# A Fourier-mixing and maxout kernel: another order of loads, writes and preparations ahead of the first block

## The chip, the cores and the metric

The kernel runs on one core of a Trainium2 chip. The metric is the device time of one execution in microseconds (us), a median over runs. One execution was also recorded by the hardware profiler; its times are those of the trace below.

## The reference

The input x has 8 sequences of 3072 tokens with 256 features. The first part takes the real part of a two-dimensional Fourier transform of each sequence, the second a feed-forward layer with three input matrices and a maximum:

```python
def _attn_ref(x):                       # x: (8, 3072, 256)
    X = np.fft.fft(x, axis=1)
    X = np.fft.fft(X, axis=2)
    return X.real.astype(np.float32)

def _moe_ref(x, w1, w2, w3, w_out):     # w1, w2, w3: (256, 768), w_out: (768, 256)
    h = np.maximum(np.maximum(x @ w1, x @ w2), x @ w3)
    return (h @ w_out).astype(np.float32)
```

The output has 24576 rows of 256 in float32.

## The kernel before, in words

**The transform over the tokens** is done in two stages for each sequence ("block", b from 0 to 7). A token index is split as 32 rows (a) by 96 columns (s); by symmetry only 49 columns (NS) are kept, with the mirrored ones stacked on other partitions. `load_x` fetches x into the tile xt, two loads (h = 0, 1) for each range of columns; `mirror` (lines 126 and 127, DVE) folds the features in half on the second 64 partitions. `Mix.s(k)` multiplies eight columns by the small table tabz (two matmuls of 512 columns) and evicts them on ScalarE (ACT) to the tile tb; s0 to s6 cover the 49 columns. `Mix.y` writes tb to a DRAM buffer db, one DMA for the even and one for the odd columns; `Mix.z` reads it back in another layout, as the tile yb with 98 partitions. So a transposition goes through DRAM. `Mix.u` and `Mix.x0` make a correction for feature 0, which `Mix.c` copies into yb. `Mix.k(which, g)` multiplies yb by a third of the table te_tab or to_tab (1536 columns, in thirds g = 0, 1, 2) and evicts the result to tE or tO. `Mix.end` makes the middle token.

**The tables** are computed on the chip: `angles(c0, c1)` computes angles on DVE for a range of the columns (four instructions), `tables(c0, c1)` makes two sines and an absolute value of them on ACT.

**The transform over the features** is multiplied into the weights once. `product(i, half, jh, ...)` is four matmuls of 384 columns; `keep_product` evicts them: half 0 to gE on DVE or another engine, half 1 to gO on ACT, from which gD is scaled. jh is the half of the 768 hidden columns. The products of jh = 0 come ahead of block 0, those of jh = 1 are the four steps of `prep_first` inside it. `prep_second` has four steps: three times four matmuls with an eviction to g1t, and then twelve matmuls that give gw, with which the linear part of the layer is computed. `load_w(jh)` loads w1, w2, w3 as two halves, from POOL's queue.

**The main loop** runs over 8 blocks, each with three groups (blk) of six units (jc): 18 units a block. A unit is `unit_plus` (four matmuls of 512 columns into the accumulators pse2 and pse3, lines 390 and 391) and `unit_out` (a ReLU of pse2 on ACT into stmp, then a maximum with pse3 on DVE, into hp). One unit later `finish` adds `unit_minus` (two matmuls with gD, line 398) into the same accumulators, which gives the mirrored tokens, and takes the maximum again, into hm. There are two buffers each of pse2 and pse3, so a unit cannot begin before hm of the unit two before it is taken. The second layer's matmuls (lines 429, 437 and 414) of the group before are spread between the units; stores go out from SP's queue and, as scattered rows, from POOL's.

**What sets the order.** The order on each engine's queue is written out by hand: a list `plan` says behind which unit of which block a piece is issued, `at(b, unit, fn)` fills it. Engines run their queues in order; waits are put in by the framework from what is read and written. PSUM has eight banks: ps_f (two buffers) for s, k, x0, end and the preparations' outputs inside the blocks, ps_s (six buffers) only at the beginning, then handed over to the accumulators and to ps_o. The tile warm is in ps_s; `warm_up(n)` issues n matmuls whose result nobody reads. Before the change they multiply the first columns of x:

```python
    def warm_up(n):
        for _ in range(n):
            nc.tensor.matmul(warm, tab_at[0], xt[0][:, 0:8:2, 0:128], start=True, stop=True)
```

For block 0 the loads of x come in four ranges of columns, FIRST = ((0, 16), (16, 32), (32, 40), (40, 49)), and the writes `Mix.y` in the same four. The zeros of the tile zero are written to the end of each row of db once, at the start.

Of the kernel before, what the change touches and what calls it, by code (L numbers as in the profile page):

```python
# [50 lines left out]
def kernel(  # L51
# [123 lines left out]
    zero = gen.tile([128, 256], BF16, tag="zero")  # L175
    nc.vector.memset(zero, 0.0)
    for db in dbs:
        pads = db[:, 64 * 128:].rearrange("s (r c) -> s r c", c=256)
        nc.sync.dma_start(out=pads, in_=zero[0:NS].unsqueeze(1).to_broadcast([NS, 2, 256]))
# [79 lines left out]

    def tables(c0, c1):  # L260
        cs = slice(c0, c1)
        nc.scalar.activation(out=te_tab[:, cs], in_=kvec[:, cs], func=AX.Sin, scale=step)
        nc.scalar.activation(out=q[:, cs], in_=kvec[:, cs], func=AX.Abs)
        nc.scalar.activation(out=to_tab[:, cs], in_=q[:, cs], func=AX.Sin, scale=-step,
                             bias=half_pi)
# [13 lines left out]
    def keep_product(psg, i, half, jh, evict_e):  # L279

        cs = slice(jh * 384, (jh + 1) * 384)
        if half == 0:
            evict_e(out=gE[i][:, cs], in_=psg[:, 0:384])
        else:
            nc.scalar.copy(out=gO[i][:, cs], in_=psg[:, 0:384])
            nc.gpsimd.tensor_scalar(out=gD[i][:, cs], in0=gO[i][:, cs], scalar1=dif,
                                    scalar2=None, op0=ALU.mult)
# [33 lines left out]
    class Mix:  # L321
# [19 lines left out]
        def y(self, s0=0, s1=NS):  # L341
            dst = self.db.rearrange("s (q f) -> q s f", f=128)
            done = []
            for hh in range(2):
                n = (s1 - s0 + 1 - hh) // 2
                done.append(nc.sync.dma_start(
                    out=dst[0:64, s0 + hh:s1:2, :],
                    in_=tbv[hh * 64:hh * 64 + 64, s0 // 2:s0 // 2 + n, :]))
            return done

        def z(self, i0=0, i1=RI, eng=nc.sync):
            rows = self.db.rearrange("s (c q) -> (s c) q", c=2)
            return eng.dma_start(out=yb[0:KS, i0 * 256:i1 * 256], in_=rows[:, i0 * 256:i1 * 256])
# [14 lines left out]
        def k(self, which, g):  # L368
# [6 lines left out]
            nc.scalar.copy(out=(self.tE, self.tO)[which][:, g * 512:(g + 1) * 512], in_=ps2)  # L375
# [159 lines left out]
    def warm_up(n):  # L535
        for _ in range(n):
            nc.tensor.matmul(warm, tab_at[0], xt[0][:, 0:8:2, 0:128], start=True, stop=True)
# [7 lines left out]
    m = Mix(0)  # L545
    m.s(0, pool=ps_s)
    m.s(1, pool=ps_s)
    m.y(0, 16)
    warm_up(3)
# [3 lines left out]
    warm_up(3)  # L553
    m.s(4, pool=ps_s)
    m.y(32, 40)
    warm_up(2)
    m.s(5, pool=ps_s)
    m.s(6, pool=ps_s)
    written = m.y(40, NS)
# [5 lines left out]
    m.z(0, 6)  # L565
    m.z(6, RI)
    load_w(1, written[-1])
    warm_up(4)
# [5 lines left out]
    warm_up(8)  # L574
# [6 lines left out]
    for u in range(3):  # L581
# [10 lines left out]
    nc.gpsimd.dma_start(out=wout_bf.rearrange("p (jc c) -> p jc c", jc=NJC),  # L592
                              in_=moe_w_out.rearrange("(jc p) c -> p jc c", jc=NJC))
    HALVES = ((0, 25), (25, NS))
    for (s0, s1) in HALVES:
        for h in range(2):
            load_x(1, s0, s1, h)

# [7 lines left out]

    m.c(0, 6, nc.scalar.copy)
    m.k(0, 0)
    m.k(1, 0)
# [41 lines left out]
    for (u, fn) in ((1, lambda: next(first)), (1, lambda: next(first)),  # L651
                    (2, lambda: next(first)), (2, lambda: next(first)), (2, lambda: m.c(6, RI)),
                    (2, lambda: m.k(0, 1)), (2, lambda: tables(1024, NHALF + 1)),
                    (3, lambda: m.k(1, 1)), (3, lambda: next(second)), (4, lambda: next(second)),
                    (4, lambda: next(second)), (5, lambda: next(second)),
# [13 lines left out]
    ahead0 = {5: ("s0", "s1"), 6: ("s2", "y0"), 7: ("s3", "s4", "u"), 8: ("s5", "s6", "y1", "x"),  # L669
# [82 lines left out]
```

## Time and profile before

| | |
|---|---|
| median of 3 runs | 422.1 us (421.14 to 423.2) |
| the profiled execution | 420.71 us, of which span 418.9 us |
| mean granted TensorE clock | 0.998 |
| TensorE (PE) busy | 394.4 us, 94% of the span |
| VectorE (DVE) busy | 293.4 us, 70% |
| ScalarE (ACT) busy | 252.8 us, 60% |
| GpSimd (POOL) busy | 154.0 us, 37% |

How to read the rows shown below. In a view in order of time a row gives the start in us, the busy time in us, the engine, the line of the kernel, the operation, output<-input with shapes, how many instructions (x4), and in brackets the idle time of the engine before it with what ended that. PEld is TensorE's load of weights; SPq and POOLq are DMA issues from those queues. A matmul's end is modelled; matmuls are pipelined, so the next one starts before the listed end. In a view by stretches a row gives the stretch, its length, then for PE, PEld, DVE, ACT and POOL the busy time and the number of instructions, the granted clock, the mean share of time in which the 16 DMA engines were busy (above 1 where packets overlap), and GB/s.

### The profile page before, as it was taken

To read this page: it belongs to the slowest core of one execution; us is meant where nothing else is said; L and a number is where in the kernel's file an instruction comes from. 1 tells how busy PE (TensorE), PEld (TensorE's weight loads), DVE (VectorE), ACT (ScalarE), POOL (GpSimd) and SP (SyncE) were. 2 spreads that over 40 slices of the span, in tenths; PEclk is the share of its full clock that TensorE was granted. 3 is DMA by queue.
4 is the path that set the end of the run, shared out by engine and by line. 5 is a ranking of instruction groups with operands and counts; after the bars stand their busy time and mean duration, and the time that the engine had idled before them with its cause. 6 is when DMAs were issued, how large, how long until landed. Compare 5 with 4: busy or idle time off the path is not lost.

```text
span 418.9 us, 8123 instructions
## 1 busy us (share of the span) xinstructions
PE 394.4 (94%) x2732; PEld 247.3 (59%) x2780; DVE 293.4 (70%) x527; ACT 252.8 (60%) x475; POOL 154.0 (37%) x264
## 2 busy tenths in 40 slices
PE   1977789999999999999999999999999999999995
PEld 0334456656665666656665666656665666656664
DVE  6876556866785676856786676856786676667772
ACT  2666656665576656665576656665576656645550
POOL 7381123424532434324532434324442432333430
PEclk9999999999999999999999999999999999999999
DMA  8997237935962569335962569335982552212224
GB/s 123 171 203 124 64 71 183 194 91 113 222 150 67 136 165 199 90 88 112 227 148 64 139 160 194 98 88 115 210 163 66 136 152 75 77 57 66 83 75 125
DMA packets 66443, 53.25 MB, mean 127 GB/s; under 512 B 34661, under 2 KB 62000, under 8 KB 65204
## 3 DMA queue, kind: packets, MB, share of 16 engines
q0 software_dynamic: 23376, 26.27, 32.1%
q1 hardware_dynamic: 42386, 25.95, 23.8%
q10 hardware_dynamic: 640, 0.52, 0.5%
q8 instruction: 21, 0.34, 0.3%
q14 instruction: 20, 0.16, 0.1%
HBM read 35.14 MB, written 31.69 MB: 160 GB/s over the span
## 4 chain that ended last, share of the span: by engine, by line
PE 88%; DVE 4%; DMA 3%; ACT 2%; issue 1%; POOL 1%; DVEq 0%; POOLq 0%; SPq 0%; ACTq 0%
PE po L414 29%; PE pse L390 16%; PE pse L398 14%; PE pse L391 13%; PE ps L333 5%; PE po L437 5%; PE pl L429 3%; PE ps L373 2%; DMA xt<-in_x_dram 2%; DVE xt L126 1%; DVE hm L405 1%; DMA yb<-db 1%; DVE hp L405 1%; PE psg L273 1%; DVE xt L127 1%
## 5 line engine op out<-in xcount | busy, mean ns | idle before, releaser
L404 ACT ACTIVATE stmp<-pse 128x512 bf16<-128x512 f32 x288 | 169.9, 601 | 80.6 <-PE pse L391 60.5
L447 POOL DMA_INDIRECT out_dram<-ot,rows_m x92 | 104.0, 1131 | 236.4 <-DVE ot L442 225.2
L405 DVE TENSOR_TENSOR hp<-pse,stmp 128x512 bf16<-128x512 f32 x144 | 99.6, 691 | 109.5 <-PE pse L398 57.4
L390 PE MATMUL pse<-tE,gE 128*128 128x512 bf16 x286 | 108.4, 379 | 3.3 <-ACT stmp L404 0.9
L405 DVE TENSOR_TENSOR hm<-pse,stmp 128x512 bf16<-128x512 f32 x144 | 99.0, 688 | 1.0 <-ACT stmp L404 0.9
L391 PE MATMUL pse<-tO,gO 128*128 128x512 bf16 x251 | 95.1, 379 | 0.2
L414 PE MATMUL po<-wout_bf,hp 128*128 128x256 bf16 x576 | 86.1, 273 | 0.0
L398 PE MATMUL pse<-tO,gD 128*128 128x512 bf16 x279 | 83.8, 379 | 0.5
L414 PE MATMUL po<-wout_bf,hm 128*128 128x256 bf16 x576 | 78.6, 273 | 0.0
L414 PEld LDWEIGHTS <-hp 128*128 128x128 bf16 x576 | 56.3, 98 | 26.2
L414 PEld LDWEIGHTS <-hm 128*128 128x128 bf16 x576 | 56.3, 98 | 16.4
L442 DVE TENSOR_TENSOR ot<-po,even 128x512 f32<-128x512 f32 x92 | 62.9, 683 | 0.2
L398 PEld LDWEIGHTS <-gD 128*128 128x128 bf16 x288 | 27.6, 98 | 32.1
L335 ACT CAST tb<-ps 128x512 bf16<-128x512 f32 x48 | 26.3, 588 | 28.5 <-PE ps L333 28.5
L391 PEld LDWEIGHTS <-gO 128*128 128x128 bf16 x288 | 28.1, 97 | 23.4 <-issue 2.3
L390 PEld LDWEIGHTS <-gE 128*128 128x128 bf16 x288 | 28.1, 98 | 22.3 <-issue 0.8
L333 PE MATMUL ps<-xt,tabz 128*128 128x512 bf16 x96 | 27.0, 400 | 12.6 <-DVE xt L127 11.2
L437 PE MATMUL po<-gw,tO 128*128 128x512 bf16 x92 | 34.9, 379 | 0.0
L433 ACT COPY even<-pl 128x512 f32<-128x512 f32 x46 | 27.0, 587 | 0.0
L375 ACT CAST tO<-ps 128x512 bf16<-128x512 f32 x24 | 14.0, 585 | 16.5 <-PE ps L373 8.8
L121 POOL DMA_DIRECT2D xt<-in_x_dram x36 | 23.4, 659 | 0.0
L375 ACT CAST tE<-ps 128x512 bf16<-128x512 f32 x24 | 14.1, 587 | 14.6 <-PE ps L373 14.6
(132 smaller groups left out, 223.5 us busy)
## 6 DMA issues: line engine op xcount, KB each, us to landing
yb<-db SPq DMA_DIRECT2D x7, 833.0 KB
xt<-in_x_dram POOLq DMA_DIRECT2D x14, 384.0 KB, 8.6
out_dram<-ot SPq DMA_DIRECT2D x56, 96.0 KB, 3.8
out_dram<-ot SPq DMA_DIRECT2D x64, 64.0 KB, 3.8
db<-tb SPq DMA_DIRECT2D x21, 192.0 KB, 3.0
xt<-in_x_dram POOLq DMA_DIRECT2D x7, 400.0 KB, 6.4
xt<-in_x_dram POOLq DMA_DIRECT2D x7, 368.0 KB, 8.3
out_dram<-ot SPq DMA_DIRECT2D x64, 32.0 KB, 2.0
```

The costliest lines, as they stand in the source:

```text
L333: nc.tensor.matmul(ps1, tab_at[hh], self.x[:, 8 * k + hh:8 * k + 8:2, 0:128], start=(hh == 0), stop=(hh == 1))
L375: nc.scalar.copy(out=(self.tE, self.tO)[which][:, g * 512:(g + 1) * 512], in_=ps2)
L390: nc.tensor.matmul(pse[:, 0:n], gE[i][:, js], te, start=True, stop=False)
L391: nc.tensor.matmul(pse[:, 0:n], gO[i][:, js], to, start=False, stop=True)
L398: nc.tensor.matmul(pse, gD[i][:, js], to, start=False, stop=True, skip_group_check=True)
L404: nc.scalar.activation(out=stmp[:, 0:n], in_=pses[0][:, 0:n], func=AX.Relu)
L405: nc.vector.tensor_tensor(out=dst, in0=src3, in1=stmp[:, 0:n], op=ALU.max)
L414: nc.tensor.matmul(po, hcols(jc), wout_bf[:, jc * 256:(jc + 1) * 256], start=False, stop=(jc == NJC - 1), skip_group_check=True)
L433: nc.scalar.copy(out=even, in_=pl)
L437: nc.tensor.matmul(po, to[:, cp], gw[:, 256:768], start=True, stop=True)
L442: nc.vector.tensor_tensor(out=ot.rearrange("p (h c) -> p h c", h=2), in0=po.rearrange("p (h c) -> p h c", h=2), in1=lin.unsqueeze(1).to_br ...
L447: stored(nc.gpsimd.indirect_dma_start(out, bass.IndirectOffsetOnAxis(ap=rows_m[0:128 - lo, b * 12 + slot: b * 12 + slot + 1], axis=0), ot[ ...
```

## The change

It touches the beginning, up to unit 8 of block 0, and the column of block 0 in the list for block 1's s stage:

- `warm_up` multiplies the tile zero, which grows from 256 to 512 columns, instead of x. 11 such matmuls stand ahead of s0, 4 between s1 and s2, 6 behind the products; those between s3, s4, s5 and behind x0 are gone (before: 3, 3, 2, 4 and 8). The DMA that writes the zeros to db reads them without a broadcast.
- Block 0 writes db in three ranges of columns, (0, 16), (16, 32), (32, 49), six DMAs in place of eight; the odd columns of the last range are issued from ACT's queue, behind the last eviction.
- The first read, 6 of 17 parts of each row, is cut in three by rows: columns 0 to 31 (64 partitions), column 48 (2), columns 32 to 47 (32).
- `load_w(1)` waits for the last of these reads, not for the last write, and w_out and block 1's x are issued directly behind it on POOL's queue, ahead of the products.
- gD is scaled on DVE instead of POOL, at once behind the gE or gO eviction.
- The copy c for the first 6 parts and k(0, 0) and k(1, 0) are issued ahead of the third `angles` and of the computation of the rows for the scattered stores; k(0, 0) is evicted on DVE, k(1, 0) on ACT as before.
- In block 0 the first step of `prep_second` and the rest of c come behind unit 0; k(0, 1) goes from unit 2 to 3, k(1, 1) from 3 to 4; the third `tables` is split into its three instructions behind units 3, 4 and 5; the further steps of `prep_second` come behind units 3, 4 and 5, one each (before: 3, 4, 4, 5). Block 1's s1 goes from unit 5 to 6.

The matmuls that compute something are the same in number and shape.

```diff
-    zero = gen.tile([128, 256], BF16, tag="zero")
+    zero = gen.tile([128, 512], BF16, tag="zero")
...
-        nc.sync.dma_start(out=pads, in_=zero[0:NS].unsqueeze(1).to_broadcast([NS, 2, 256]))
+        nc.sync.dma_start(out=pads, in_=zero[0:NS].rearrange("p (r c) -> p r c", c=256))
...
+    def table(k, c0=1024, c1=NHALF + 1):
+        cs = slice(c0, c1)
+        if k == 0:
+            nc.scalar.activation(out=te_tab[:, cs], in_=kvec[:, cs], func=AX.Sin, scale=step)
+        elif k == 1:
+            nc.scalar.activation(out=q[:, cs], in_=kvec[:, cs], func=AX.Abs)
+        else:
+            nc.scalar.activation(out=to_tab[:, cs], in_=q[:, cs], func=AX.Sin, scale=-step,
+                                 bias=half_pi)
+
     def tables(c0, c1):
...
+        for k in range(3):
+            table(k, c0, c1)
...
-            nc.gpsimd.tensor_scalar(out=gD[i][:, cs], in0=gO[i][:, cs], scalar1=dif,
+            nc.vector.tensor_scalar(out=gD[i][:, cs], in0=gO[i][:, cs], scalar1=dif,
...
-        def y(self, s0=0, s1=NS):
+        def y(self, s0=0, s1=NS, second=nc.sync):
...
-                done.append(nc.sync.dma_start(
+                done.append((nc.sync, second)[hh].dma_start(
...
-        def z(self, i0=0, i1=RI, eng=nc.sync):
+        def z(self, i0=0, i1=RI, s0=0, s1=NS):
             rows = self.db.rearrange("s (c q) -> (s c) q", c=2)
-            return eng.dma_start(out=yb[0:KS, i0 * 256:i1 * 256], in_=rows[:, i0 * 256:i1 * 256])
+            return nc.sync.dma_start(out=yb[2 * s0:2 * s1, i0 * 256:i1 * 256],
+                                     in_=rows[2 * s0:2 * s1, i0 * 256:i1 * 256])
...
-        def k(self, which, g):
+        def k(self, which, g, evict=nc.scalar.copy):
...
-            nc.scalar.copy(out=(self.tE, self.tO)[which][:, g * 512:(g + 1) * 512], in_=ps2)
+            evict(out=(self.tE, self.tO)[which][:, g * 512:(g + 1) * 512], in_=ps2)
...
-            nc.tensor.matmul(warm, tab_at[0], xt[0][:, 0:8:2, 0:128], start=True, stop=True)
+            nc.tensor.matmul(warm, zero[:, 0:128], zero, start=True, stop=True)
...
     m = Mix(0)
+    warm_up(11)
     m.s(0, pool=ps_s)
     m.s(1, pool=ps_s)
     m.y(0, 16)
-    warm_up(3)
+    warm_up(4)
     m.s(2, pool=ps_s)
     m.s(3, pool=ps_s)
     m.y(16, 32)
-    warm_up(3)
     m.s(4, pool=ps_s)
-    m.y(32, 40)
-    warm_up(2)
     m.s(5, pool=ps_s)
     m.s(6, pool=ps_s)
-    written = m.y(40, NS)
+    m.y(32, NS, nc.scalar)
...
-    m.z(0, 6)
+    m.z(0, 6, 0, 32)
+    m.z(0, 6, 48, NS)
+    landed = m.z(0, 6, 32, 48)
     m.z(6, RI)
-    load_w(1, written[-1])
-    warm_up(4)
+    load_w(1, landed)
+    nc.gpsimd.dma_start(out=wout_bf.rearrange("p (jc c) -> p jc c", jc=NJC),
+                        in_=moe_w_out.rearrange("(jc p) c -> p jc c", jc=NJC))
+    HALVES = ((0, 25), (25, NS))
+    for (s0, s1) in HALVES:
+        for h in range(2):
+            load_x(1, s0, s1, h)
     for half in range(2):
         keep_product(product(0, half, 0, ps_f, "ps"), 0, half, 0, dve)
     tables(512, 1024)
     for half in range(2):
         keep_product(product(1, half, 0, ps_s, "ps"), 1, half, 0, dve)
-    warm_up(8)
+    warm_up(6)
+    m.c(0, 6, nc.scalar.copy)
+    m.k(0, 0, dve)
+    m.k(1, 0)
     angles(1024, NHALF + 1)
...
-    for (u, fn) in ((1, lambda: next(first)), (1, lambda: next(first)),
-                    (2, lambda: next(first)), (2, lambda: next(first)), (2, lambda: m.c(6, RI)),
-                    (2, lambda: m.k(0, 1)), (2, lambda: tables(1024, NHALF + 1)),
-                    (3, lambda: m.k(1, 1)), (3, lambda: next(second)), (4, lambda: next(second)),
-                    (4, lambda: next(second)), (5, lambda: next(second)),
+    for (u, fn) in ((0, lambda: next(second)), (0, lambda: m.c(6, RI)),
+                    (1, lambda: next(first)), (1, lambda: next(first)),
+                    (2, lambda: next(first)), (2, lambda: next(first)),
+                    (3, lambda: m.k(0, 1)), (3, lambda: table(0)), (3, lambda: next(second)),
+                    (4, lambda: m.k(1, 1)), (4, lambda: table(1)), (4, lambda: next(second)),
+                    (5, lambda: table(2)), (5, lambda: next(second)),
                     (7, lambda: m.k(0, 2)), (8, lambda: m.k(1, 2)), (8, m.end)):
...
-    ahead0 = {5: ("s0", "s1"), 6: ("s2", "y0"), 7: ("s3", "s4", "u"), 8: ("s5", "s6", "y1", "x"),
+    ahead0 = {5: ("s0",), 6: ("s1", "s2", "y0"), 7: ("s3", "s4", "u"), 8: ("s5", "s6", "y1", "x"),
```

More of the change, by code (lines that the diff above doesn't have):

```diff
@@ L258, in angles @@
         _reduce(nc, kvec[:, cs], kvec[:, cs], q[:, cs], 3072.0)
-    def tables(c0, c1):
[L261 to L265, printed above, removed]
+    def table(k, c0=1024, c1=NHALF + 1):
[7 more added lines that the diff above has]
+                                 bias=half_pi)
+    def tables(c0, c1):
+        for k in range(3):
+            table(k, c0, c1)
     def product(i, half, jh, pool, tag):
@@ L590 @@
     dve(out=rows_m, in_=rows_f)
[L592 to L597, printed above, removed]
     ps_s_cm.__exit__(None, None, None)
@@ L605 @@
     first, second = prep_first(), prep_second()
-    m.c(0, 6, nc.scalar.copy)
-    m.k(0, 0)
-    m.k(1, 0)
     mixes = {0: m}
```

## The prediction

> **What bounds the kernel now.** I read the profile's page first, then the busy time by stage, then the instructions in order of time.
>
> ```profile
> span 418.9 us, 8123 instructions
> PE 394.4 (94%) x2732; PEld 247.3 (59%) x2780; DVE 293.4 (70%) x527; ACT 252.8 (60%) x475; POOL 154.0 (37%) x264
> ...
> 24.00:56.00 32.00, 25.47 (x174) 14.65 (x179) 19.51 (x41) 20.21 (x39) 9.36 (x13) 1.00 0.63 109
> 56.00:400.00 344.00, 341.73 (x2398) 216.85 (x2441) 244.83 (x402) 217.16 (x407) 126.89 (x215) 1.00 0.55 128
> ```
>
> The last two rows are stretches of time, with PE's busy time behind the length. From 56 us to 400 us TensorE has work for 341.7 of 344 us. It has 24.5 us without work in all, nearly all before 56 us. The change touches only that part, so whatever block 0 gains or loses by 56 us arrives unchanged at the end. The profiled execution took 420.71 us (span plus 1.8 us); the median of the runs is 422.1 us. I work out a difference and take it from the median.
>
> **The first block's preparations, up to the first unit.** All of these wait for the first transposition through DRAM.
>
> ```profile
> 1.47 0.17 DVE L176 MEMSET zero<- 128x128 uint32 x1
> 8.98 1.87 PE L333 MATMUL ps<-xt,tabz 128*128 128x512 bf16 x4 [8.98 <-DVE xt L127]
> 14.12 0.17 DVE L127 COPY xt<-xt 64x9 bf16<-64x9 bf16 x1
> 15.89 0.60 PE L333 MATMUL ps<-xt,tabz 128*128 128x512 bf16 x2
> 17.01 0.26 ACT L339 CAST tb<-ps 64x128 bf16<-64x128 f32 x1
> 18.44 0.62 SPq L346 DMA_DIRECT2D db<-tb  x1
> 20.67 0.34 SPq L353 DMA_DIRECT2D yb<-db  x1
> 24.16 0.40 PE L373 MATMUL ps<-te_tab,yb 98*128 98x96 bf16 x6 [1.62 <-DMA yb<-db]
> ```
>
> The mirror copies end at 14.29, yet PE reaches s5 only at 15.89: cold matmuls and eight filling ones stand between. In the changed kernel 11 matmuls on zeros start as soon as zeros exist, and between s2 and s6 none is left. So s5 follows the last mirror at 14.3, and with 0.6 for two matmuls, 0.58 and 0.26 for the evictions the last eviction ends near 15.9 instead of 17.27: 1.4 us earlier. Twice the zeros make the early memset up to 0.17 us longer, hidden because DVE then waits for x.
>
> Then the writes. SP issues eight, the last at 18.44; it lands at 20.67.
>
> ```profile
> 17.00:18.00 1.00, 0.63 (x4) 0.11 (x2) 0.96 (x3) 1.00 (x4) 0.00 (x0) 1.00 0.97 211
> 18.00:19.00 1.00, 0.98 (x6) 0.41 (x5) 0.94 (x3) 1.00 (x4) 0.00 (x0) 1.00 0.45 90
> 19.00:20.00 1.00, 1.00 (x8) 0.59 (x6) 0.96 (x2) 0.97 (x2) 0.00 (x0) 1.00 0.60 129
> 20.00:20.60 0.60, 0.60 (x6) 0.39 (x4) 0.53 (x5) 0.60 (x3) 0.00 (x0) 1.00 0.16 31
> ```
>
> The second-last column is the DMA engines' share: full until 18 us, then 0.45 + 0.60 + 0.6 x 0.16 = 1.15 us of work stretched over 2.6 us, since each issue costs SP 0.62 us. Six writes, the last two issued at 16.0 on SP and ScalarE side by side, keep the engines full, so the data land up to 1.45 us earlier, at 19.2. The first read part (64 of 98 rows, which needs only the first two writes) now runs among them; I allow 0.5 us and take 19.7. Bounds: 18.2 (16.0 plus the 2.2 from issue to landing above) and 20.7 (as now). ScalarE's own issue (0.62) is hidden: its tables wait for DVE's angles anyway.
>
> Behind the last write come a two-row and a 32-row read. One issue costs 0.34. The 98-row read took 24.16 - 20.67 = 3.45 us; the lower bound for a small transfer is the write's 2.2. A third of the rows lies nearer to the lower: 2.5. So the first read is complete at 19.7 + 0.35 + 2.5 = 22.6 instead of 24.16: 1.6 us earlier (range 21.9 to 23.9).
>
> ```profile
> 22.25 0.46 ACT L285 CAST gO<-psg 128x384 bf16<-128x384 f32 x1
> 24.14 0.22 ACT L366 COPY yb<-x0s 98x6 bf16<-98x6 bf16 x1 [1.43 <-DMA yb<-db]
> 25.08 0.59 ACT L375 CAST tO<-ps 128x512 bf16<-128x512 f32 x1
> ```
>
> More would not help: ScalarE's queue, fixed by DVE's angles and not by the reads, is free for the 0.22 us copy at 22.7. So k(0,0) starts at 22.6, k(1,0) at 22.9. DVE evicts the first, ScalarE the second, side by side. The first unit starts near 23.8 with all operands, against 25.67: a gain of 1.8 us at this point.
>
> **What is late next: DVE.** The eviction of k(0,0) stands in DVE's queue ahead of the third angles and the store rows. Until now these ran inside the wait for the read.
>
> ```profile
> 15.86 0.55 DVE L194 TENSOR_SCALAR kvec<-kvec,s_of,phi 128x512 f32<-128x512 f32 x1
> 17.36 0.69 DVE L26 TENSOR_TENSOR kvec<-kvec,q 128x512 f32<-128x512 f32 x1
> ...
> 21.44 0.54 DVE L194 TENSOR_SCALAR kvec<-kvec,s_of,phi 128x513 f32<-128x513 f32 x1
> 23.45 0.95 DVE L26 TENSOR_TENSOR kvec<-kvec,q 128x513 f32<-128x513 f32 x1
> 24.32 0.30 DVE L194 TENSOR_SCALAR adj<-pidx 128x4 f32<-128x4 f32 x3
> 25.50 0.32 DVE L590 CAST rows_m<-rows_f 128x96 int32<-128x96 f32 x1
> ```
>
> The 512-column angles took 15.86 to 18.05 = 2.2 us, those of 513 columns 21.44 to 24.40 = 2.95 us while POOL was scaling weights and issuing loads beside them. POOL no longer scales, but still issues; I take 2.5 and keep both ends. The store rows take 24.32 to 25.82 = 1.5 us.
>
> ```profile
> 16.44 0.43 DVE L22 TENSOR_SCALAR q<-kvec 128x512 f32<-128x512 f32 x1
> 26.77 0.69 DVE L405 TENSOR_TENSOR hp<-pse,stmp 128x512 bf16<-128x512 f32 x1 [0.95 <-ACT stmp L404]
> 27.84 0.48 PE L273 MATMUL psg<-w_bf,md_all 128*128 128x384 bf16 x2
> 34.19 0.60 PE L303 MATMUL pst<-md_all,w_bf 128*128 128x256 bf16 x4
> ```
>
> DVE's new order: the eviction (0.69, as the nearest row from PSUM) from 23.1, where k(0,0) has ended, to 23.75; angles to 26.25; store rows to 27.75; hp of unit 0 to 28.45. PE has unit 0, the first step of prep_second and unit 1 to do. Two matmuls of 512 columns are listed at 0.60, one at 0.38, so the next starts 0.22 after one; the four of 256 columns above give 0.11. That is 0.87 + 0.44 + 0.87, and one minus matmul, to 26.2. Unit 0's second minus matmul waits for that hp, because both use pse3. PE stands still for 2.2 us, and the first product of prep_first starts at 28.45 + 0.25 = 28.7, where it started at 27.84. So this point is 0.9 us later, not earlier, with 0.4 us of work already behind it: the gain of 1.8 us is used up here. With the ends of the angles it is 28.4 to 29.2.
>
> The two scalings of the first weight halves on DVE lie in its wait for k(0,0) and cost nothing (uncovered, up to 0.43 each, the wider row above); the two of the other halves add between 0 and 0.43 each to units 1 and 2, inside hp's waits, and take 1.24 us off POOL each.
>
> **The loads that POOL issues.** The other halves of w1, w2, w3 now wait for the read (22.6), not for the last write.
>
> ```profile
> 20.89 2.18 POOL L155 DMA_DIRECT2D w_bf<-in_moe_w_dram  x3 [6.28 <-DMA db<-tb]
> 23.10 2.66 POOL L286 TENSOR_SCALAR gD<-gO,dif 128x384 bf16<-128x384 bf16 x2
> ```
>
> The product needs w2, the second of the three: issued at 22.6 + 0.75 = 23.35. From issue to landing, by two answers of the view by tile, first for the w tiles, then for x:
>
> ```profile
> DMA to landing us min/median/max: 6.4/6.9/8.0
> ```
> ```profile
> DMA to landing us min/median/max: 4.4/7.4/11.2
> ```
>
> Until now the w loads shared the engines with the large second read; issued after it they should come nearer to x's minimum. With 4.4 w2 lands at 27.8, with 6.4 at 29.8; I take 5.1: 28.45, just ahead of DVE. wout and x of block 1 follow without gD between them, from 24.8 instead of 25.7, so neither gets later.
>
> **Block 0 after the first product.** The stalls of PE on the way to 56 us:
>
> ```profile
> 33.98 0.37 PE L373 MATMUL ps<-to_tab,yb 98*128 98x96 bf16 x5 [0.53 <-POOL yb L366]
> 35.72 0.38 PE L390 MATMUL pse<-tE,gE 128*128 128x512 bf16 x1 [0.93 <-ACT stmp L404]
> 36.56 0.38 PE L390 MATMUL pse<-tE,gE 128*128 128x512 bf16 x1 [0.46 <-DVE hm L405]
> 43.34 0.61 PE L333 MATMUL ps<-xt,tabz 128*128 128x512 bf16 x2 [1.79 <-DVE xt L127]
> 50.55 0.60 PE L333 MATMUL ps<-xt,tabz 128*128 128x512 bf16 x2 [0.71 <-ACT tb L335]
> ```
>
> The first is POOL's copy c behind its gD; c is now issued in unit 0 and POOL is free. The next two are ScalarE doing a gO, k(0,1) and three tables in one go in unit 2; these are spread over units 3 to 5. The fourth is s1 waiting for a mirror in the same unit; s1 moves one unit back. The idle times in brackets count from a matmul's listed end, 0.16 after the next could have started, so 3.7 + 4 x 0.16 = 4.3 us; the third row follows a matmul missing from the records (0.2 less): 4.1 go. New ones: s2 behind s1 needs a ps_f buffer that ScalarE must first empty (0.7, as the last row, which stays), and hm of two units is late (0.4 together, by the third row). So 1.1 come; bounds 0 and 2.2, twice that.
>
> **Sum.** First product +0.9; work done before it -0.4; stalls gone -4.1; new +1.1: -2.5 us. 422.1 - 2.5 = 419.6 us; the profiled execution would be 418.2.
>
> **The rivals.** *Nothing gained by splitting the read:* the parts share the same engines, so the last part lands 3.45 us after its issue as the whole did, at 23.5, and everything above shifts by 0.9: -1.6, 420.5 us. For it: the read's time may be mostly fixed; against: the share of 1.15 in 2.6 us shows engines waiting, not full. If w2 then also takes 6.4, it lands at 30.7, 2.0 after the product of the sum, which leaves -0.5: 421.6. The Trainium skill ("DMA: Bandwidth & Descriptors", Rules for kernel authors) speaks for this rival: two transfers to disjoint partition halves serialize on the same engines, and should be one. The trace agrees that reads and writes share engines, but here a part starts earlier because it waits for less, which the rule does not weigh.
>
> *The filling matmuls fill nothing:* started when the memset of zeros ends, near 1.7, 11 at 0.43 (four took 1.87 at 8.98, the last with its tail) end at 6.4, and PE is idle for 2.6 us until 8.98. If it is cold again there, s0 to s3 run as now, the last eviction ends at up to 16.7, and the path loses 0.2 to 0.8: -1.7 to -2.3, about 420.1. The trace shows a gap of 1.79 us, with two matmuls at full speed (0.61) behind it, and none of 2.6. The Trainium skill ("TensorE: Matmul & The Clock Gate", Part 1) puts the loss of the clock at an idle window of about 3.4 us; by that it stays warm, which no row here shows.
>
> *Slower:* the weight loads become the bound. POOL now issues eight loads back to back behind the second read, and w2 could take as long as the slowest x load in such a queue, 11.2 us: 23.35 + 11.2 = 34.55, the product 5.85 us later than in the sum: +3.3, 425.4 us. PE has nothing else to do then, since unit 1 is followed by the products. The gain is gone once w2 takes over 7.9 us from its issue. Against it: the w loads' own maximum is 8.0, for the first halves, issued right behind block 0's x.
>
> **How the numbers follow.** A measurement of this kernel tells about 0.5% (2.1 us) from no change; below 420.0 us is faster, above 424.2 slower. The forecast with its bounds (first product 28.4 to 29.2, new stalls 0.3 to 1.3) gives -2.0 to -3.6, nearly all of it below 420.0, chance 0.62. The split that gains nothing 0.24 (-0.5 to -1.6) and the cold clock 0.06 (about -2) are within 0.5%. The late weights have 0.08, of which 0.01 ends within 0.5%. So faster 0.62, same 0.31, slower 0.07. The range holds the forecast's cases from -3.6, and on the other side the second case to -0.5, with 0.6 for the scatter of the runs: 417.9 to 422.2 us.
>
> **What the profile after will show.** Right: eviction of s6 near 15.9, last write landing before 20, k(0,0) at 22.6, DVE without a gap from tE to hp at 28.45, PE's one stall of 2.2 us on that hp, no stall of over 1 us between 33 and 46 us, and PE dense from 53.5. Wrong: k(0,0) after 23.3 (writes or reads mis-sized); PE's stall ended by a w load; new stalls on ScalarE or DVE of over 1.5 us together; or a loss after 56 us, which nothing here expects.

## The result, and the profile after

The changed kernel takes 419.06 us (median of 5 runs, 418.11 to 420.11) where the kernel before takes 422.07 us beside it: 0.9927 of the time, 95% interval 0.9900 to 0.9955, so 3.1 us less. (The ratio is not formed from these two medians, so it can differ a little from their quotient.) The forecast was 419.6 us, faster, range 417.9 to 422.2. The profiled execution took 418.23 us, of which 416.5 are the span (forecast 418.2).

The page of the changed kernel, and its busy time by stage:

```profile
span 416.5 us, 8175 instructions
PE 401.0 (96%) x2781; PEld 249.0 (60%) x2781; DVE 294.6 (71%) x532; ACT 252.2 (61%) x474; POOL 148.8 (36%) x260
```
```profile
24.00:56.00 32.00, 27.41 (x182) 15.67 (x182) 23.70 (x50) 20.96 (x41) 6.37 (x11) 1.00 0.66 110
56.00:400.00 344.00, 344.00 (x2443) 217.09 (x2441) 244.94 (x403) 217.00 (x406) 126.88 (x215) 1.00 0.55 128
```

Nothing has changed behind 56 us: from psx of block 1, shown below, to the end of the span it is 363.2 us before and 363.3 after. The larger PE figures there (344.00 for 341.73, x2443 for x2398) are matmul records that the trace of before had lost. Between 24 and 56 us PE works 27.41 us instead of 25.47.

Two points show where the time came from, first in the kernel before, in order of time: the start of the first unit, and psx of block 1 (the matmuls of its correction for feature 0), behind which PE is dense in both kernels.

```profile
25.24 0.38 PE L390 MATMUL pse<-tE,gE 128*128 128x512 bf16 x1 [0.42 <-ACT tE L375]
55.73 0.22 PE L361 MATMUL psx<-tabx,x0u 128*98 128x17 bf16 x2 [0.62 <-ACT tb L335]
```

The same view of the changed kernel, its engines in turn (ACT, SP, POOL, DVE, PE):

```profile
15.92 0.27 ACT L346 CAST tb<-ps 64x128 bf16<-64x128 f32 x1
16.06 0.70 ACTq L353 DMA_DIRECT2D db<-tb  x1
22.88 0.22 ACT L374 COPY yb<-x0s 98x6 bf16<-98x6 bf16 x1
18.81 1.99 SPq L360 DMA_DIRECT2D yb<-db  x4
23.06 2.18 POOL L155 DMA_DIRECT2D w_bf<-in_moe_w_dram  x3 [8.66 <-DMA yb<-db]
23.68 0.69 DVE L383 CAST tE<-ps 128x512 bf16<-128x512 f32 x1 [0.53 <-PE ps L381]
24.29 0.54 DVE L194 TENSOR_SCALAR kvec<-kvec,s_of,phi 128x513 f32<-128x513 f32 x1
26.37 0.69 DVE L26 TENSOR_TENSOR kvec<-kvec,q 128x513 f32<-128x513 f32 x1
27.99 0.21 DVE L606 CAST rows_m<-rows_f 128x96 int32<-128x96 f32 x1
28.11 0.68 DVE L413 TENSOR_TENSOR hp<-pse,stmp 128x512 bf16<-128x512 f32 x1
21.96 1.46 PE L545 MATMUL warm<-zero 128*128 128x512 bf16 x6
23.25 0.39 PE L381 MATMUL ps<-te_tab,yb 98*128 98x96 bf16 x6
24.43 0.38 PE L398 MATMUL pse<-tE,gE 128*128 128x512 bf16 x1 [0.54 <-DVE tE L383]
28.85 0.38 PE L406 MATMUL pse<-tO,gD 128*128 128x512 bf16 x1 [1.89 <-DVE hp L413]
29.07 0.49 PE L280 MATMUL psg<-w_bf,md_all 128*128 128x384 bf16 x2
48.02 0.60 PE L340 MATMUL ps<-xt,tabz 128*128 128x512 bf16 x2 [0.71 <-ACT tb L342]
51.94 0.59 PE L340 MATMUL ps<-xt,tabz 128*128 128x512 bf16 x2 [0.64 <-ACT tO L383]
53.20 0.22 PE L369 MATMUL psx<-tabx,x0u 128*98 128x17 bf16 x2 [0.62 <-ACT tb L342]
```

The reader is to see four things. k(0,0) starts at 23.25 straight behind the six filling matmuls: PE did not wait for the read, which ScalarE's copy, starting at 22.88, already has. The first unit starts 0.81 us earlier (24.43 for 25.24). DVE then works without a gap from tE to hp, and PE waits 1.89 us for that hp, so the first product of prep_first starts 1.23 us *later* than before (29.07 for 27.84). And from there to psx it takes 24.13 us instead of 27.89: of the stalls of 0.53, 0.93, 0.46 and 1.79 us none is left, and only the last three rows, which were there before, still show a wait. The whole gain arises between the first product and psx.

### The profile page after: what moved, and what is told of

The parts are those of the page before. It is cut to its first block, busy times and chain, and to the rows that moved or that the text cites. A ratio compares the mean times of both kernels' runs of the same rounds, so it can differ in the third digit from the quotient of the medians.

```text
span 416.5 us, 8175 instructions
## 1 busy us (share of the span) xinstructions
PE 401.0 (96%) x2781; PEld 249.0 (60%) x2781; DVE 294.6 (71%) x532; ACT 252.2 (61%) x474; POOL 148.8 (36%) x260
## 4 chain that ended last, share of the span: by engine, by line
PE 93%; DVE 2%; ACT 2%; DMA 1%; issue 0%; POOL 0%; ACTq 0%; DVEq 0%; POOLq 0%
PE po L422 30%; PE pse L398 15%; PE pse L406 15%; PE pse L399 15%; PE ps L340 5%; PE po L445 5%; PE ps L381 3%; PE pl L437 2%; PE psg L280 2%; DMA xt<-in_x_dram 1%; PE warm L545 1%; ACT stmp L412 1%; ACT tb L342 1%; DVE hm L413 0%; PE psw L319 0%
## 5 line engine op out<-in xcount | busy, mean ns | idle before, releaser
L399 PE MATMUL pse<-tO,gO 128*128 128x512 bf16 x288 | 109.0, 379 | 0.0
L406 PE MATMUL pse<-tO,gD 128*128 128x512 bf16 x288 | 85.8, 379 | 1.9 <-DVE hp L413 1.9
L398 PEld LDWEIGHTS <-gE 128*128 128x128 bf16 x288 | 28.2, 98 | 22.2 <-issue 0.4
L121 POOL DMA_DIRECT2D xt<-in_x_dram x36 | 23.4, 656 | 0.0
L126 DVE COPY xt<-xt 64x1524 bf16<-64x1524 bf16 (+4 forms) x32 | 19.1, 598 | 4.5 <-DMA xt<-in_x_dram 3.7
```

What stands on the lines that cost most here:

```text
L398: nc.tensor.matmul(pse[:, 0:n], gE[i][:, js], te, start=True, stop=False)
L399: nc.tensor.matmul(pse[:, 0:n], gO[i][:, js], to, start=False, stop=True)
L406: nc.tensor.matmul(pse, gD[i][:, js], to, start=False, stop=True, skip_group_check=True)
```

## The experiments

**The theory.** The order of block 0's preparations brings the gain; the new beginning (filling, writes, read parts, scalings on DVE) brings the read forward, and DVE's queue takes that back. Rivals: the beginning carries the gain; the split read does; the filling matmuls do; the loads of weights set the first product.

All twelve runs and the two kernels, with two starts from each profile and two differences, in us: k(0,0) is the first matmul that needs the read, "first product" the first of prep_first. The medians of the kernel before beside the three groups were 420.52, 421.96 and 421.24 us.

| kernel | median | ratio to before (95%) | k(0,0) | first product | from k(0,0) to it | from it to psx |
|---|---|---|---|---|---|---|
| before | 422.07 | 1 | 24.16 | 27.84 | 3.68 | 27.89 |
| changed | 419.06 | 0.9927 (0.9900 to 0.9955) | 23.25 | 29.07 | 5.82 | 24.13 |
| plan_only | 418.66 | 0.9954 (0.9931 to 0.9977) | 25.06 | 29.00 | 3.94 | 24.15 |
| start_only | 422.94 | 1.0049 (1.0025 to 1.0073) | 22.69 | 28.84 | 6.15 | 28.77 |
| rows_early | 417.58 | 0.9914 (0.9887 to 0.9941) | 24.03 | 28.78 | 4.75 | 24.15 |
| no_fill | 417.75 | 0.9932 (0.9910 to 0.9954) | 22.41 | 28.56 | 6.15 | 24.14 |
| after_again | 418.43 | 0.9917 (0.9885 to 0.9948) | 21.68 | 27.84 | 6.16 | 24.14 |
| angles_wait | 417.13 | 0.9886 (0.9853 to 0.9919) | 23.11 | 27.07 | 3.96 | 24.97 |
| angles_wait_w | 416.53 | 0.9875 (0.9843 to 0.9906) | 23.14 | 27.07 | 3.93 | 24.14 |
| one_read | 418.23 | 0.9913 (0.9883 to 0.9944) | 22.93 | 28.43 | 5.50 | 24.13 |
| plan_only_again | 417.37 | 0.9918 (0.9893 to 0.9944) | 23.51 | 27.45 | 3.94 | 24.14 |
| wait_w_nofill | 417.19 | 0.9910 (0.9876 to 0.9943) | 22.68 | 27.43 | 4.75 | 24.14 |
| gd_pool | 422.40 | 1.0026 (1.0005 to 1.0046) | 22.23 | 30.96 | 8.73 | 25.31 |
| four_writes | 418.81 | 0.9945 (0.9918 to 0.9971) | 23.19 | 28.61 | 5.42 | 24.15 |

The right-hand column repeats to 0.02 us in the ten profiles with the new order in which neither a weight nor a scaling is late. The column before it does not repeat so well: 3.94 twice for plan_only, but 5.42 to 6.16 for the six kernels with the changed DVE queue. In the three at 6.15 and 6.16 k(0,0) came early, and its eviction on DVE stood behind the second scaling, which waits for ScalarE's gO; in the two lowest (one_read, four_writes) the angles took 2.4 us instead of 2.7 to 2.8. k(0,0) itself moves by over 2 us between profiles of the same beginning. So a difference tells something where it is larger than this spread; a single k(0,0) carries no verdict.

### The order alone, and the beginning alone

plan_only takes the kernel before and gives it the changed plan; start_only takes the changed kernel and gives it the old plan (ahead0 goes with it in both):

```diff
-    for (u, fn) in ((1, lambda: next(first)), (1, lambda: next(first)),
-                    (2, lambda: next(first)), (2, lambda: next(first)), (2, lambda: m.c(6, RI)),
-                    (2, lambda: m.k(0, 1)), (2, lambda: tables(1024, NHALF + 1)),
...
+    for (u, fn) in ((0, lambda: next(second)), (0, lambda: m.c(6, RI)),
+                    (1, lambda: next(first)), (1, lambda: next(first)),
+                    (2, lambda: next(first)), (2, lambda: next(first)),
+                    (3, lambda: m.k(0, 1)), (3, lambda: table(0)), (3, lambda: next(second)),
...
```

> The kernel before with the new order of block 0's preparations alone (plan, single tables, s1 one unit later); loads, writes, reads, gD on POOL, filling matmuls as before. Theory (the net gain comes from the stalls that the new order removes; the earlier start is paid back in DVE's queue): first product of prep_first stays near 27.84 us (up to 28.2, one step of prep_second more ahead of it), the stalls of 0.93 at 35.7 and 1.79 at 43.3 us are gone, time 2.4 to 3.4 us less than the kernel before, about 419.1. Rival A (the earlier start carries the gain, the order little): at most 1.3 us less, 420.8 or above. Rival B (start and order need each other, since POOL still scales gD): no gain, 421.5 to 422.5.

> The changed kernel with the old order of block 0's preparations (plan tuple and s0, s1 in unit 5 as before): the new beginning alone. Theory: the first unit starts at 24.4 us instead of 25.2, but the first product waits for DVE's hp as in the changed kernel, near 29.1 instead of 27.84, with about 0.4 us of work moved ahead of it, and the stalls of block 0 stay: 0.5 to 1.8 us slower than the kernel before, about 423. Rival A (the start carries the gain): 0.8 to 1.8 us faster, 420.3 to 421.3. Rival B: no difference, 421.8 to 422.4.

> The new order of block 0 alone, once more, beside the three below on one chip. Theory (the beginning as made is paid back by DVE's queue, so that the order alone gives nearly all): 0.993 to 0.996 of the kernel before, and over the kernel whose DVE queue is kept clear (wait_w_nofill) by 2.0 to 3.5 us, which is what the beginning is worth when nothing takes it back. Rival (the order alone gives all that there is, and the beginning nothing in any order): within 1 us of wait_w_nofill.

plan_only came out 1.9 us faster than before, and in the second group 3.5 us (by the ratios, 0.46% and 0.82%), below the theory's 2.4 to 3.4 once and just above it once. k(0,0), which waits for the read in both profiles, starts 1.55 us apart (25.06 and 23.51): in the first s4 and the filling behind it ran cold (matmuls of 512 columns 0.43 us apart instead of 0.22) and the eviction of s6 ended at 18.83 instead of 16.87. That is the size of the difference between the two times, but one profile of each does not show that it is its cause. What doesn't differ is the rest: 3.94 us to the first product and 24.15 to psx, both times. start_only is 2.1 us slower than before (interval 1.1 to 3.1), a little above the theory's 0.5 to 1.8, and rules out that the beginning carries the gain by itself. Its stalls in order of time:

```profile
28.62 0.38 PE L406 MATMUL pse<-tO,gD 128*128 128x512 bf16 x1 [2.24 <-DVE hp L413]
36.73 0.38 PE L398 MATMUL pse<-tE,gE 128*128 128x512 bf16 x1 [1.64 <-ACT stmp L412]
45.22 0.61 PE L340 MATMUL ps<-xt,tabz 128*128 128x512 bf16 x2 [1.11 <-DVE xt L127]
```

The first is the price of DVE's new queue, the others are the old plan's: ScalarE's group in unit 2 and the mirror. Behind the second the clock is at half for 3.4 us, which can account for the stretch to psx (28.77) being longer than before's 27.89.

The last comparison of the expectation went against the theory. Beside wait_w_nofill, whose DVE queue is clear, plan_only_again is not 2.0 to 3.5 us slower but level (417.37 and 417.19). Why, stands with wait_w_nofill below. So the rival of that expectation, a beginning that gives nothing in any order, is not refuted: only angles_wait_w (0.9875) came out faster, in another group, and its interval overlaps that of plan_only_again.

### DVE's queue

rows_early moves the nine small operations for the store rows ahead of the second pair of products, where DVE waits:

```diff
     for half in range(2):
         keep_product(product(0, half, 0, ps_f, "ps"), 0, half, 0, dve)
+    rows_v = rows_f.rearrange("p (b r) -> p b r", r=12)
+    ...
+    dve(out=rows_m, in_=rows_f)
     tables(512, 1024)
```

> The changed kernel with the nine small DVE operations for the store rows moved between the first and the second pair of first products, where DVE waits; the third angles stay. Theory (DVE's queue between the eviction of k(0,0) and unit 0's hp sets the first product): hp of unit 0 starts 1.0 to 1.3 us earlier, near 27.0; the first product then waits for hp and for the weight w2 (28.16 in the changed kernel), so it starts near 28.2 instead of 29.07: 0.8 to 1.1 us less than the changed kernel, about 418.1. Rival (the weights or the clock set the first product): within 0.3 us of the changed kernel. Rival (delayed evictions of gE[1] hold up unit 0): first unit later than 24.43 by 0.3 or more, no gain.

k(0,0) came 0.8 us later in this profile than in the changed kernel's, so the starts of hp (27.83) and of the first product (28.78) missed the expected 27.0 and 28.2. The read was not the reason: POOL's loads, which it releases, start earlier here (22.69 for 23.06). PE was still busy, with products at half the clock and with the six filling matmuls, one of which is missing from the records:

```profile
21.62 0.85 PE L280 MATMUL psg<-w_bf,nmd_all 128*128 128x384 bf16 x2
22.26 1.93 PE L545 MATMUL warm<-zero 128*128 128x512 bf16 x5
24.03 0.39 PE L381 MATMUL ps<-te_tab,yb 98*128 98x96 bf16 x6
22.69 2.17 POOL L155 DMA_DIRECT2D w_bf<-in_moe_w_dram  x3 [7.99 <-DMA yb<-db]
```

From k(0,0) to the first product it takes 4.75 us, 1.07 less than the changed kernel's 5.82, about the length of the operations moved; against all six profiles with the changed queue it is 0.67 to 1.41 less. The time (0.9914) can't be told from the changed kernel's.

angles_wait moves the third angles as well, back into the wait for the read, with k(0,0) evicted by ScalarE; angles_wait_w also lets the weights go at the last write:

```diff
-    for half in range(2):
-        keep_product(product(1, half, 0, ps_s, "ps"), 1, half, 0, dve)
+    keep_product(product(1, 0, 0, ps_s, "ps"), 1, 0, 0, dve)
+    angles(1024, NHALF + 1)
+    ...                              # the store rows
+    keep_product(product(1, 1, 0, ps_s, "ps"), 1, 1, 0, dve)
...
-    m.k(0, 0, dve)
+    m.k(0, 0)
...
-    load_w(1, landed)                # angles_wait_w only
+    load_w(1, written[0])
```

> The changed kernel with the third angles and the store rows moved back into DVE's wait for the read (between gE[1] and the second scaling), and k(0,0) evicted by ScalarE again, so that DVE has neither of them ahead of unit 0's hp. Theory (DVE's queue sets the first product): hp of unit 0 near 25.9 us instead of 28.11; the next to come late is the weight w2, which lands near 28.2, and ends PE's stall; first product near 28.2, 0.8 to 1.1 us less than the changed kernel. Rival (DVE's new order is not the limit): within 0.3 us. Rival (two evictions one behind the other on ScalarE hold up unit 0): first unit 0.6 later, first product no earlier.

> As angles_wait, and the second halves of w1, w2, w3 released by the last write on SP, as in the kernel before, instead of the read: they are issued near 20 us and share the engines with the reads. Theory (after DVE the weights are the limit): w2 lands before 27, first product 26.9 to 27.6, 1.5 to 2.3 us less than the changed kernel. Rival (the loads slow the reads as much as they gain): k(0,0) 0.5 to 1.5 us later than 23.25, first product 28 or later, no better than angles_wait.

angles_wait in order of time:

```profile
25.70 0.69 DVE L413 TENSOR_TENSOR hp<-pse,stmp 128x512 bf16<-128x512 f32 x1
27.07 0.48 PE L280 MATMUL psg<-w_bf,md_all 128*128 128x384 bf16 x2
30.48 0.50 PE L280 MATMUL psg<-w_bf,md_all 128*128 128x384 bf16 x2 [0.65 <-DMA w_bf<-in_moe_w_dram]
```

hp starts at 25.70 instead of 28.11, PE's stall on it is gone, and the first product starts at 27.07, 2.0 us earlier than in the changed kernel with the same k(0,0) (23.11 and 23.25). That DVE's queue set it is shown. What comes late next is a weight load, as expected, but not w2: that had landed by 27.07. The third product, which needs w3, waits 0.65 us at 30.48, and the stretch to psx grows from 24.14 to 24.97. With the weights released earlier that wait goes too:

```profile
23.14 0.39 PE L381 MATMUL ps<-te_tab,yb 98*128 98x96 bf16 x6 [1.90 <-DMA yb<-db]
27.07 0.49 PE L280 MATMUL psg<-w_bf,md_all 128*128 128x384 bf16 x2
29.66 0.49 PE L280 MATMUL psg<-w_bf,md_all 128*128 128x384 bf16 x2
19.66 2.17 POOL L155 DMA_DIRECT2D w_bf<-in_moe_w_dram  x3 [5.08 <-DMA db<-tb]
```

These are rows of angles_wait_w. The loads go at 19.66 instead of 22.45, and k(0,0) is not later for it (23.14 for 23.11). The read itself is: PE waits 1.90 us for it here, while in angles_wait it was complete before POOL's loads at 22.45, and PE was held until 23.11 by its filling matmuls. In wait_w_nofill, with the loads at 20.40, k(0,0) starts at 22.68 without waiting for the read, so whether the loads delay the read stays open. angles_wait_w is the fastest of all, 0.9875 of before: 416.53 us (416.36 to 417.81) where the changed kernel takes 418.43 (417.04 to 420.77) beside it; the intervals of the two ratios still overlap.

### The parts of the beginning

```diff
-    warm_up(11)                      # no_fill, wait_w_nofill: 11, 4 and 6 left out
...
-    m.z(0, 6, 0, 32)                 # one_read
-    m.z(0, 6, 48, NS)
-    landed = m.z(0, 6, 32, 48)
+    landed = m.z(0, 6)
...
+    m.y(32, 40)                      # four_writes: behind s4
...
-    m.y(32, NS, nc.scalar)
+    m.y(40, NS)
...
-            nc.vector.tensor_scalar(out=gD   # gd_pool
+            nc.gpsimd.tensor_scalar(out=gD
```

> The changed kernel without any filling matmul (11, 4 and 6 left out). Theory (the early 11 bought nothing: the clock was cold at 9.0 us and again at 18 us, and ScalarE and the reads set the path): s6's eviction ends 0 to 0.8 us later than 16.19, the first unit 0 to 0.5 us later than 24.43, where DVE's queue absorbs most of it: 0 to 0.5 us over the changed kernel, 419.1 to 419.6. Rival (the filling keeps the clock up and that carries part of the gain): s and the first products all at 0.43 us, first unit 1 us or more later, 0.8 to 1.5 us over the changed kernel, 420 or above.

> The changed kernel with one 98-row first read behind all writes instead of the three row parts. Theory (the read matters only as it moves k(0,0), and DVE's queue behind it goes with it one to one; three parts cost two more issues of 0.35 us and end with the same last part): k(0,0) between 0.5 us earlier and 0.5 later than 23.25, time within 0.5 us of the changed kernel. Rival (the split brings the read forward): the read takes 3.45 us from the last write's landing near 19.8 plus 0.3, k(0,0) at 23.6 to 24.2, 0.4 to 0.9 us over the changed kernel.

> The changed kernel with the writes as before: eight, all issued by SP (rows 32 to 40 and 40 to 49 apart), the read in three parts behind them. Theory (each issue costs SP 0.62 us, and the reads stand behind): last write issued near 18 instead of 16.1, k(0,0) 0.5 to 1.2 us later than in the changed kernel, and the time with it, 0.4 to 1.2 us over. Rival (the engines are the limit, not the issues): k(0,0) within 0.4 us, time within 0.4 us of the changed kernel.

> The changed kernel itself once more, beside the three below on one chip: every theory expects its own ratio again, 0.990 to 0.9955 of the kernel before.

no_fill leaves out all filling and is as fast as the changed kernel (0.9932 and 0.9927). one_read is as fast too (418.23 and 418.43 beside it). Neither part has a value in time that can be measured.

The split does seem to bring the read forward. From the end of the eviction of s6 to POOL's loads, which the read releases, it takes 5.71 to 6.87 us in the seven profiles with six writes, a split read and such loads, and 7.45 us in one_read (one profile). k(0,0) does not show it (22.93 in one_read, 21.68 to 24.03 with the split), since in five of the seven profiles with split and filling PE comes to k(0,0) only when the read is already there.

four_writes is inconclusive: SP's last issue ends at 18.85 instead of 16.87, but k(0,0) at 23.19 lies in the same range, and the ratio (0.9945) is up by 0.2 to 0.3% with overlapping intervals.

The profile of after_again shows why an early read is worth little. Its read is the earliest of all:

```profile
21.68 0.39 PE L381 MATMUL ps<-te_tab,yb 98*128 98x96 bf16 x6 [0.89 <-DMA yb<-db]
22.25 0.40 PE L381 MATMUL ps<-to_tab,yb 98*128 98x96 bf16 x6 [0.18 <-ACT yb L374]
27.62 0.38 PE L406 MATMUL pse<-tO,gD 128*128 128x512 bf16 x1 [1.80 <-DVE hp L413]
65.05 0.40 PE L381 MATMUL ps<-te_tab,yb 98*128 98x96 bf16 x6 [0.91 <-DMA yb<-db]
```

It repeats the ratio (0.9917). k(1,0) waits for ScalarE's copy, the first product for DVE's hp, and in block 1 PE waits 0.91 us for the next read, which it did not in the first profile. psx comes 1.22 us earlier than there (51.98 for 53.20), and yet the span is only 0.2 us shorter (416.3 for 416.5).

> The changed kernel with the four scalings of weight copies (gD) on POOL again; the loads that were moved ahead of them stay ahead. Theory (in POOL's queue they now stand behind seven or eight loads): the two first scalings run from about 28.5 to 31 us, unit 0's minus matmuls wait for them, the first product comes 1.5 to 2.5 us later than 29.07 or 27.84, 420 to 421 us, 1.5 to 2.3 over the changed kernel. Rival (the scaling is off the path, and only DVE's or POOL's occupation changes): within 0.5 us of the changed kernel.

gd_pool is slower than the kernel before, and its loss of some 1% against the changed kernel is twice what was expected:

```profile
28.00 2.50 POOL L293 TENSOR_SCALAR gD<-gO,dif 128x384 bf16<-128x384 bf16 x2
29.34 0.39 PE L406 MATMUL pse<-tO,gD 128*128 128x512 bf16 x1 [3.18 <-POOL gD L293]
30.56 0.61 PE L406 MATMUL pse<-tO,gD 128*128 128x512 bf16 x1 [0.83 <-POOL gD L293]
30.96 0.85 PE L280 MATMUL psg<-w_bf,md_all 128*128 128x384 bf16 x2
```

The place is as the theory put it: the scalings stand behind the loads in POOL's queue and run from 28.00 to 30.50. Beyond the delay of the first product (30.96), the products behind this wait run at half the clock (the next row of two starts at 31.60, 0.64 later, where it is 0.33 elsewhere), and the stretch to psx is 1.2 us longer. So the scaling on DVE, which by itself costs little, is what the loads' move ahead of it needs.

> angles_wait_w without any filling matmul. Theory (the filling buys nothing that lasts): 0.985 to 0.9895 of the kernel before, like angles_wait_w; s6's eviction within 0.8 us of 15.7. Rival (filling matmuls carry the early start here, where nothing downstream hides it): 0.8 to 1.5 us over angles_wait_w, 0.990 to 0.992.

wait_w_nofill is angles_wait_w without its three calls of filling. It came out at 0.9910, in the rival's range, with an interval (0.9876 to 0.9943) that reaches into the theory's too. Its profile has two late points: s2 to s5 run cold, so that the eviction of s6 ends at 16.97 instead of 15.68, and the products ahead of block 0 run at half the clock:

```profile
12.69 3.50 PE L340 MATMUL ps<-xt,tabz 128*128 128x512 bf16 x8 [2.26 <-DVE xt L127]
19.48 0.85 PE L280 MATMUL psg<-w_bf,nmd_all 128*128 128x384 bf16 x2
23.57 0.40 PE L381 MATMUL ps<-to_tab,yb 98*128 98x96 bf16 x6 [0.43 <-ACT yb L374]
```

ScalarE is late by these 1.3 us, k(1,0) waits for its copy, and the first product of prep_first comes at 27.43. Whether filling pays once DVE's queue is clear (0.36 us in this pair of profiles) stays open.

## Why the prediction was right, point by point

**The bound.** PE is dense behind 56 us, and all that changed lies before: shown by the stages.

**The beginning.** The eviction of s6 ends at 16.19 (forecast 15.9), the read is complete by 22.88, where ScalarE's copy starts (22.6, range 21.9 to 23.9). Over the seven profiles with six writes, a split read and filling k(0,0) starts at 22.88 on average (21.68 to 24.03), over the three with the old beginning at 24.24 (23.51 to 25.06): 1.4 us earlier, forecast 1.6. The first unit at 24.43 is later than the forecast 23.8. At most 0.3 of that is the read. The other 0.4 is a term that the prediction left out: six filling matmuls stand in PE's queue ahead of k(0,0) and hold it until 23.25. DVE's eviction moved with it, to 23.68 to 24.37 instead of 23.1 to 23.75.

**DVE late next.** This step decided the sign at the first product, and it held: tE, the angles (24.29 to 27.06, 2.77 us for 2.5), the store rows (1.05 us up to hp, for 1.5), hp ending at 28.79 (28.45), PE's stall 1.89 us (2.2) on it, the first product at 29.07 (28.7). The experiments show the mechanism: with the store rows out of that queue the way from k(0,0) to the first product is 0.7 to 1.4 us shorter, with the angles out as well 1.5 to 2.2 us (3.96 and 3.93 for 5.42 to 6.16), and PE's stall is gone. The beginning as made gives nothing that these measurements resolve: 0.9954 and 0.9918 for the order alone, 0.9927 and 0.9917 with the beginning.

**Block 0.** From the first product to psx the forecast was -0.4 - 4.1 + 1.1 = -3.4 us. Measured: 27.89 to 24.13, -3.76. The sum is right to 0.36 us; the new stalls are probably the term that was too large (1.1), since between 30 and 46 us no wait of PE is long enough to be listed. At psx the gain in the profile is 2.53 us where 2.5 was forecast. That it agrees so closely is luck: the first product came 0.33 us later than forecast, and the stretch behind it was shorter by 0.36. The small end of the forecast's spread, -2.0, is -1.8 by the ends that it names (first product at 29.2, new stalls 1.3).

**The scalings on DVE** took 0.32 us each, lay in its wait and cost nothing in this profile, as forecast. Where k(0,0) came early they did cost something: in after_again the second ran from 22.12 to 22.64 and held up the eviction of k(0,0). The prediction priced what they add but not what they allow: on POOL, behind the loads moved ahead of them, they would have cost some 1% (gd_pool).

**The rivals.** *Late weights* did not occur; the first product waited for hp. But their margin was thin: as soon as hp came earlier, w3 was late. *Nothing gained by splitting*: its mechanism did not occur. The last part, issued at 20.05, was complete by 22.88, 2.8 us later and not 3.45, while one_read's whole read, issued at 19.33, took 3.6 us until k(0,0). In time the split is worth nothing all the same, as one_read shows. The Trainium skill ("DMA: Bandwidth & Descriptors", Rules for kernel authors) advises one transfer instead of two to disjoint partition halves; one_read, as fast with one, agrees in time.

*The filling matmuls fill nothing* got 0.06 and is what the profile shows:

```profile
1.84 4.87 PE L545 MATMUL warm<-zero 128*128 128x512 bf16 x11 [1.84 <-DVE zero L176]
9.00 1.86 PE L340 MATMUL ps<-xt,tabz 128*128 128x512 bf16 x4 [2.28 <-DVE xt L127]
17.50 0.50 PE L280 MATMUL psg<-w_bf,md_all 128*128 128x384 bf16 x2 [2.03 <-ACT md_all L566]
18.63 0.85 PE L280 MATMUL psg<-w_bf,md_all 128*128 128x384 bf16 x2
```

The four matmuls at 9.00 took 1.86 us as before. Only its price was wrong: no_fill shows no loss that can be measured, and by the profiles ScalarE's tables and DVE's queue came later behind it. The step that failed is the chance given to this case, drawn from one gap of 1.79 us.

## What to carry to other kernels

When a wait is shortened, look at what had been running inside it: here 3.8 us of DVE work had been free in the wait for the read, and behind the read it cost 1.9 us (5.87 for 3.94 on average from k(0,0) to the first product), more than the 1.4 us by which k(0,0) came earlier. Change the order of the queues and the start apart from each other before keeping both. Compare differences between two points of one profile rather than absolute times, and learn first how far a difference itself scatters: here 0.02 us behind the first product, but 0.7 us ahead of it. Before the first matmul behind a transfer is taken for its arrival, look whether the engine waited for it at all. A small operation moved to another engine may cost nothing and still be indispensable, if it lets other work in its old queue go ahead.

## What the runs showed of the hardware that was not expected

**The clock.** The changed kernel in stretches, the third column from the right being the granted clock; PE had idled 2.03 us until 17.50:

```profile
17.00:18.00 1.00, 0.50 (x2) 0.11 (x2) 0.97 (x3) 1.00 (x4) 0.00 (x0) 1.00 0.95 201
18.00:19.00 1.00, 0.98 (x4) 0.48 (x5) 0.93 (x3) 1.00 (x3) 0.00 (x0) 0.50 0.93 190
20.00:21.00 1.00, 1.00 (x5) 0.49 (x4) 0.93 (x5) 0.84 (x2) 0.00 (x0) 0.50 0.71 200
21.00:22.00 1.00, 1.00 (x7) 0.51 (x6) 0.63 (x2) 0.97 (x3) 0.00 (x0) 0.79 0.91 174
```

Half the clock lasts here from 18.0 to 21.4, that is 3.4 us, while PE is fully busy. Cut into half microseconds, all nine profiles with the 11 early matmuls show such a stretch ahead of the first unit, four of 6.8 us (start_only, rows_early, gd_pool, four_writes; rows_early has another of 3.4) and five of 3.4; the two without filling have one of 3.4, at 23.4 and 19.4 us; the three with the old beginning have none. start_only and gd_pool have one more in block 0, from 37.5 and 29.9 us, behind stalls of 1.64 and 3.18 us: these two cost their length and then a slow stretch, while the changed kernel's stall of 1.89 us (until 28.85) and start_only's of 2.24 us (until 28.62) had none behind them. The granted clock also reads 1.00 where matmuls are 0.43 us apart (9 to 12 us in the changed kernel), so a cold start is read from the spacing.

The early matmuls didn't even buy a warm start reliably: of the same 11, the four matmuls behind them ran hot in four profiles (1.02 to 1.11 us, idle before them 2.13 to 2.23 us), cold in four (1.86 to 1.87 us, idle 1.80 to 2.80 us), and between in one. The four that were hot are those that then had 6.8 us at half the clock. The Trainium skill ("TensorE: Matmul & The Clock Gate", Part 1) has the clock decided in windows of about 3.4 us that run free of the kernel, with a varying number of cold matmuls; the lengths of 3.4 and 6.8 us and the split of four and four agree. It also has the clock fall after an idle window of about 3.4 us; here it fell behind 2.03 and 1.64 us, so by these runs less will do. The length of the idle time alone does not decide it: behind 1.97 us ahead of the same products it fell in wait_w_nofill and did not in after_again, angles_wait_w and one_read. What does was not found.

**One small scaling on two engines.** 128x384 in bf16 took 0.32 us on DVE and 1.25 us on POOL.
